# Strided attention blocks transposed in pairs, their value products on both row halves, and a smaller first transfer

## The chip, the cores and the metric

The kernel runs on one core of a Trainium2 chip. The metric is device time in microseconds (us) of one execution; lower is better. TensorE is PE in the profile (PEld is its weight load), VectorE is DVE, ScalarE is ACT, GpSimd is POOL and SyncE is SP.

## The reference

Three layers follow one another; all of it is float32, with batch 4, 8 heads, 576 positions, head size 64, model width 512 and hidden width 1024.

```
scores = where(mask, q k^T / sqrt(64), -1e9); attn = softmax(scores); x = attn v
    heads 0-3, local:   0 <= i - j < 32
    heads 4-7, strided: i >= j and i % 32 == j % 32
xk, xr = mixes of x and x shifted by one position
x2 = sigmoid(xr w_r) * (relu(xk w_k)^2 w_v)
h = relu(x2 w_in); out = (h * sigmoid(conv3(h))) w_out
```

## The kernel before, in words

Only the blocks of scores that the masks leave are computed. A local head has 9 blocks of 64 queries by 96 keys. For a strided head the positions are regrouped by remainder: 3 remainders of 18 positions make one block of 54 by 54, and a head has 11 of these. Heads go in pairs `p` (0 and 1 local, 2 and 3 strided), one head on partitions 0 to 63, the other on 64 to 127. A pair is worked in two units (`unit`, L359): 5 and 4 blocks if local, 6 and 5 if strided. So there are 8 units in each of the 4 batches, 4 of them strided.

The steps of a unit are: scores into one PSUM bank (L389), mask and row minimum on DVE (L402), exponentials on ACT (L407), sums and normalisation on DVE (L420 to L422), one transpose of each block on PE (L429) in two sections with one PSUM bank ("tr", of which there are two) each, a copy of each section to `pt` in SBUF (L432, by the helper's L258 on ACT or L260 on DVE), the value products into the one "pv" bank (L439), and the copy of their result into `xT` (L444 local; `place`, L456 and L458, strided). In a strided unit the value products contract over 54 rows, which all lie on partitions 0 to 53; `vt` holds v for one half of the blocks, so that a strided pair has two loads of it.

The two layers behind it split each float32 operand into a high and a low float32r part and take three products; these products (`mm`, L529, then `hh` L738 and `oo` L770) are most of PE's work. Weights come as 64-bit words and are narrowed by integer operations on DVE (L278 to L280) and ACT or DVE (L273, L275).

The order of the first part (attention and the layer with w_k, w_v and w_r) is written by a planner (`Plan`, L64): it gives each job the time that constants in the code say, and always takes the job that can start first. Jobs that ACT or DVE can do go to the one that is free first; from `PREFER_FROM` of the planner's time on, DVE has a handicap of 0.5. Each engine then executes its own list in that order. While nothing else is there at the beginning, PE does idle products ("stir", L648): `WARM` of them first, then some in gaps. The input transfer of the first pair is cut in two, so that the first unit's data come first (L344, L346). The second part (w_in, convolution, w_out) is a plan of its own.

Of the kernel before, what the change touches and what calls it, by code (L numbers as in the profile page):

```python
# [14 lines left out]
P = 128  # L15
# [20 lines left out]
BANKED = {"sc", "tr", "pv", "mm"}  # L36
RIGHT = {"raw", "wt", "wb", "qk", "vt", "pr", "nmx", "sums", "rec", "pt"}
# [168 lines left out]
def block_kernel(ctx, tc, qkL, qkS, vL, vS, mu_k, mu_r, w_k, w_v, w_r, w_in, conv_w, w_out, ident, mask_l, mask_s, out):  # L206
# [152 lines left out]
    def unit(b, p, half, loaded):  # L359

# [5 lines left out]
        if local:  # L366
            masks = [ml_sb[:, 0 if first + j == 0 else 1] for j in range(nb)]
            mask = fixed["ml"]
            qo = [LQ * j if half == 0 else LQ * LB[0] + S + STRIDE + LQ * j for j in range(nb)]
            ko = [LQ * LB[0] + LQ * (first + j) for j in range(nb)]  # L370
# [12 lines left out]
        pt = space(at, "pt", [P, SB[0] * SR], bufs=2, parts=2)  # L383

        def scores(e, blocks):
            for j in blocks:
                for ab in range(2):
                    r = slice(64 * ab, 64 * ab + 64)
                    pe.matmul(bank()[r, j * nk:(j + 1) * nk], qk()[r, qo[j]:qo[j] + LQ], qk()[r, ko[j]:ko[j] + nk], start=True, stop=True)  # L389

        reads = [(qk, 0)] if local and not half else [qk]
        cost = 0.025 + nk * 0.00065
        if b == 0 and p == 0 and half == 0:
            for s_ in range(2):
                plan.add({"PE": len(sections[s_]) * cost}, lambda e, s_=s_: scores(e, sections[s_]), reads, [(bank, s_)])
        else:
            first_scores.append(plan.add({"PE": nb * cost}, lambda e: scores(e, range(nb)), reads, [bank]))
        for s_, blocks in enumerate(sections):
            def masked(e, blocks=blocks):
                for i in blocks:  # L400
                    k = slice(i * nk, (i + 1) * nk)
                    dve.tensor_tensor_reduce(pr()[:, k], bank()[:, k], masks[i], -1.0 / 8.0, 3.0e38, ALU.add, ALU.min, nmx()[:, i:i + 1])  # L402

            def exps(e, blocks=blocks):
                for i in blocks:
                    k = slice(i * nk, (i + 1) * nk)
# [3 lines left out]
            plan.add({"DVE": m * (0.077 + nk / 960)}, masked, [(bank, s_), mask], [(pr, s_), (nmx, s_)])  # L410
            j = plan.add({"ACT": m * (0.29 + nk / 1400)}, exps, [(pr, s_), (nmx, s_)], [(pr, s_), (sums, s_)], table="exp")
            if unit_before[0]:
                plan.order(unit_before[0], j)
            unit_before[0] = j

        def normalise(e):
            x = pr()[:, :nb * nk].rearrange("p (n k) -> p n k", n=nb)
# [5 lines left out]
        for s_, blocks in enumerate(sections):  # L423
            turned = space(ps, "tr", [P, 512], bufs=BANKS["tr"])
            m = len(blocks)

            def turn(e, blocks=blocks, turned=turned):
                for j, i in enumerate(blocks):
                    pe.transpose(turned()[:nk, j * rows:(j + 1) * rows], pr()[:rows, i * nk:(i + 1) * nk], id_sb[:rows, :rows])  # L429

            plan.add({"PE": m * 0.098}, turn, [(pr, s_), fixed["id"]], [turned])
            copy(lambda blocks=blocks: pt()[:nk, blocks[0] * rows:(blocks[-1] + 1) * rows], lambda m=m, turned=turned: turned()[:nk, :m * rows], m * rows, [turned], [(pt, s_)])  # L432
        out_ = space(ps, "pv", [P, 512], bufs=BANKS["pv"])

        def values(e):
            for j in range(nb):
                for ab in range(2):
                    r, o = slice(64 * ab, 64 * ab + 64), j * rows + 64 * ab
                    pe.matmul(out_()[r, j * nq:(j + 1) * nq], vt()[:nk, j, r], pt()[:nk, o:o + nq], start=True, stop=True)  # L439

        plan.add({"PE": nb * (0.025 + nq * 0.00055)}, values, [vt, pt], [out_])
        x, n = xT[b], nb * nq
        if local:
            copy(lambda: x()[:, p, 1 + first * nq:1 + (first + nb) * nq], lambda: out_()[:, :n], n, [out_], [(x, 2 * p + half)])  # L444
        else:

            groups = [(0, nb, 0)] if half == 0 else [(0, nb - 1, 0), (nb - 1, 1, 1)]

            def place(e):
                dst = x()[:, p, 1:].rearrange("p (i r) -> p i r", r=STRIDE)  # L450
                src_ = out_()[:, :n].rearrange("p (n i g) -> p n i g", n=nb, i=NI)
                for j0, m, g0 in groups:
                    r0 = 3 * (first + j0)
                    d = dst[:, :, r0:r0 + m * (3 - g0)].rearrange("p i (n g) -> p n i g", n=m)
                    if e == "ACT":
                        act.activation(d, src_[:, j0:j0 + m, :, g0:], AF.Copy)  # L456
                    else:
                        dve.tensor_copy(d, src_[:, j0:j0 + m, :, g0:])  # L458

            plan.add({"ACT": 0.085 * len(groups) + n / 1400, "DVE": 0.065 * len(groups) + n / 960}, place, [out_], [(x, 2 * p + half)])  # L460

    def attention(b):
        xT[b] = space(wa, f"xT{b}", [P, KT, S + 1], tag="xT", bufs=2, parts=9)
# [352 lines left out]
def _layout(inputs):  # L816
# [9 lines left out]
        return np.ascontiguousarray(a.transpose(0, 1, 3, 2)).reshape(B, H // 4, 2 * D, -1)  # L826


    h, n0 = H // 2, LQ * LB[0]
# [9 lines left out]
    vS = v[:, h:, order].reshape(B, 2, 2, sum(SB), SQ, D).transpose(0, 1, 4, 3, 2, 5)  # L839
    vS = np.ascontiguousarray(vS).reshape(B, 2, SQ, sum(SB), 2 * D)  # L840

    t, i = np.arange(LK)[None, :], np.arange(2 * LQ)[:, None] % LQ
    near = (t > i) & (t <= i + STRIDE)
# [41 lines left out]
```

## Time and profile before

| what | us |
|---|---|
| median of 3 runs | 551.56 (550.79 to 551.92) |
| the profiled execution, its own time | 550.77 |
| its span, first to last instruction | 549.0 |
| PE busy | 536.0 |
| DVE busy | 362.3 |
| ACT busy | 350.8 |

The profile describes one execution. 1.77 us of its own time lie outside the span. A busy PE is not a PE at its peak: matmuls are pipelined, and a row's duration overlaps the next one's. What a step costs PE is therefore read from the chain of waits or from the distance of starts, not from the mean duration.

### The profile page before, as it was taken

To read this page: it belongs to the slowest core of one execution; us is meant where nothing else is said; L and a number is where in the kernel's file an instruction comes from. 1 tells how busy PE (TensorE), PEld (TensorE's weight loads), DVE (VectorE), ACT (ScalarE), POOL (GpSimd) and SP (SyncE) were. 2 spreads that over 40 slices of the span, in tenths; PEclk is the share of its full clock that TensorE was granted. 3 is DMA by queue.
4 is the path that set the end of the run, shared out by engine and by line. 5 is a ranking of instruction groups with operands and counts; after the bars stand their busy time and mean duration, and the time that the engine had idled before them with its cause. 6 is when DMAs were issued, how large, how long until landed. Compare 5 with 4: busy or idle time off the path is not lost.

```text
span 549.0 us, 11874 instructions
## 1 busy us (share of the span) xinstructions
PE 536.0 (98%) x4596; PEld 502.5 (92%) x4596; DVE 362.3 (66%) x999; ACT 350.8 (64%) x966; POOL 1.2 (0%) x15
## 2 busy tenths in 40 slices
PE   6989999999999999999999999999999999999997
PEld 5778999999999999999999999999899999998885
DVE  3999999778878757712655621699976755556510
ACT  5879998779948879927679562556554433433320
POOL 0000000000000000000000000000000000000000
PEclk9999999999999999999999999999999999999999
DMA  9764655794297440000230520323121010000011
GB/s 293 245 203 153 197 170 175 219 294 145 83 285 252 149 136 2 23 23 2 70 101 2 164 82 24 101 62 99 45 100 63 19 39 20 19 21 24 36 39 57
DMA packets 35208, 58.13 MB, mean 106 GB/s; under 512 B 3312, under 2 KB 22256, under 8 KB 35152
## 3 DMA queue, kind: packets, MB, share of 16 engines
q1 hardware_dynamic: 34576, 57.06, 32.9%
q8 instruction: 36, 0.59, 0.5%
q10 hardware_dynamic: 576, 0.32, 0.2%
q14 instruction: 20, 0.16, 0.1%
HBM read 43.74 MB, written 13.63 MB: 104 GB/s over the span
## 4 chain that ended last, share of the span: by engine, by line
PE 91%; DVE 4%; ACT 3%; DMA 1%; issue 1%; ACTq 0%
PE mm L529 44%; PE hh L738 18%; PE oo L770 18%; PE sc L389 4%; PE pv L439 3%; PE tr L429 3%; ACT pr L407 1%; DVE mx L509 1%; DVE wt L280 1%; DMA qk<-in_qkL 1%; DVE pr L402 1%; DVE wt L279 0%; ACT mx L508 0%; DVE Y L511 0%; ACT wb L273 0%
## 5 line engine op out<-in xcount | busy, mean ns | idle before, releaser
L529 PE MATMUL mm<-X,wvh 128*128 128x288 f32 x448 | 84.8, 299 | 0.0
L529 PE MATMUL mm<-Y,wkh 128*128 128x288 f32 x384 | 68.4, 296 | 0.0
L529 PEld LDWEIGHTS mm<-X,wvh 128*128 128x128 f32 x448 | 66.9, 188 | 0.5
L407 ACT ACTIVATE pr<-pr,nmx 128x54 f32<-128x54 f32 (+1 forms) x160 | 54.9, 348 | 9.4 <-DVE nmx L402 9.1
L529 PEld LDWEIGHTS mm<-Y,wkh 128*128 128x128 f32 x384 | 56.9, 188 | 0.0
L529 PE MATMUL mm<-Y,wrh 128*128 128x288 f32 x256 | 54.8, 299 | 0.6 <-DVE Y L511 0.4
L738 PE MATMUL hh<-x2h,wil 128*128 128x288 f32 x256 | 54.7, 295 | 0.0
L738 PE MATMUL hh<-x2l,wih 128*128 128x288 f32 x256 | 54.6, 294 | 0.0
L738 PE MATMUL hh<-x2h,wih 128*128 128x288 f32 x256 | 54.3, 293 | 0.0
L749 DVE SCALAR_TENSOR_TENSOR c<-hb,cw_sb,c 128x576 f32<-128x576 f32 x64 | 52.1, 818 | 1.4
L738 PEld LDWEIGHTS hh<-x2h,wih 128*128 128x128 f32 x256 | 43.9, 188 | 4.3
L529 PE MATMUL mm<-X,wvl 128*128 128x288 f32 x224 | 47.8, 295 | 0.0
L750 ACT ACTIVATE c<-c 128x576 f32<-128x576 f32 x32 | 21.9, 684 | 40.6 <-DVE c L749 40.5
L576 DVE TENSOR_TENSOR X<-sq,X 128x288 fp32r<-128x288 f32 x48 | 21.7, 458 | 35.1 <-ACT X L574 28.3
L529 PEld LDWEIGHTS mm<-Y,wrh 128*128 128x128 f32 x256 | 42.0, 188 | 1.6 <-DVE Y L511 0.6
L529 PE MATMUL mm<-Y,wkl 128*128 128x288 f32 x192 | 41.1, 295 | 0.0
L738 PEld LDWEIGHTS hh<-x2l,wih 128*128 128x128 f32 x256 | 41.0, 188 | 0.0
L738 PEld LDWEIGHTS hh<-x2h,wil 128*128 128x128 f32 x256 | 40.9, 188 | 0.0
L529 PE MATMUL mm<-Y,wrl 128*128 128x288 f32 x128 | 38.0, 297 | 0.4 <-DVE wrl L319 0.4
L746 ACT ACTIVATE hb<-hh 128x576 f32<-128x576 f32 x32 | 20.8, 651 | 24.4 <-PE hh L738 24.2
L529 PEld LDWEIGHTS mm<-X,wvl 128*128 128x128 f32 x224 | 35.9, 188 | 0.0
L751 DVE TENSOR_TENSOR c<-hb,c 128x576 f32<-128x576 f32 x32 | 24.3, 758 | 15.1 <-ACT c L750 14.6
(107 smaller groups left out, 1152.1 us busy)
## 6 DMA issues: line engine op xcount, KB each, us to landing
qk<-in_qkS SPq DMA_DIRECT2D x8, 599.0 KB
x_d<-rs SPq DMA_DIRECT2D x32, 144.0 KB
x2r<-x_d SPq DMA_DIRECT2D x8, 576.0 KB
out<-ob SPq DMA_DIRECT2D x17, 256.0 KB
qk<-in_qkL SPq DMA_DIRECT2D x7, 592.0 KB
raw<-in_w_k SPq DMA_DIRECT2D x8, 512.0 KB
raw<-in_w_v SPq DMA_DIRECT2D x8, 512.0 KB
raw<-in_w_in SPq DMA_DIRECT2D x8, 512.0 KB
```

What stands on the lines that cost most here:

```text
L389: pe.matmul(bank()[r, j * nk:(j + 1) * nk], qk()[r, qo[j]:qo[j] + LQ], qk()[r, ko[j]:ko[j] + nk], start=True, stop=True)
L407: act.activation(pr()[:, k], pr()[:, k], AF.Exp, bias=nmx()[:, i:i + 1], scale=-1.0, accum_out=sums()[:, i:i + 1])
L429: pe.transpose(turned()[:nk, j * rows:(j + 1) * rows], pr()[:rows, i * nk:(i + 1) * nk], id_sb[:rows, :rows])
L439: pe.matmul(out_()[r, j * nq:(j + 1) * nq], vt()[:nk, j, r], pt()[:nk, o:o + nq], start=True, stop=True)
L529: pe.matmul(o(), w_cols(name, j, t, part), x_[t](), start=(t == 0 and part == 0 and x_ is xhi), stop=(t == nk - 1 and x_ is xlo))
L576: plan.add({"DVE": 0.37}, lambda e: dve.tensor_tensor(l_(), sq(), h_().bitcast(F32), ALU.subtract), [sq, h_], [l_])
L738: pe.matmul(o()[:, i, :T], w()[:, t * P:(t + 1) * P], x_()[:, i, t], start=(t == 0 and w is whi and x_ is hi), stop=(t == KT - 1 and x_ is ...
L746: plan.add({"ACT": 0.54}, lambda e: act.activation(h()[:, 1:1 + S].rearrange("p (i t) -> p i t", i=2), o()[:, :, :T], AF.Relu), [o], [h])
L749: plan.add({"DVE": 0.735}, lambda e, k=k: dve.scalar_tensor_tensor(c(), h()[:, k:k + S], cw_sb[:, k * NF + f:k * NF + f + 1], c(), ALU.mul ...
L750: plan.add({"ACT": 0.6}, lambda e: act.activation(c(), c(), AF.Sigmoid), [c], [c], table="sigmoid")
L751: plan.add({"DVE": 0.67}, lambda e: dve.tensor_tensor(c(), h()[:, 1:1 + S], c(), ALU.mult), [h, c], [c])
L770: pe.matmul(o(), x_()[:, f, col:col + P], wsp["wo", f][part](), start=(f == 0 and x_ is th and part == 0), stop=(f == NF - 1 and x_ is tl))
```

## The change

Five things change.

- Strided units: a gap is left in `pr`, so that a block begins every 64 columns, and one transpose takes two neighbouring blocks (118 columns in, 118 rows out). A unit has 3 transposes, in one bank with one section, instead of 6 or 5 in two. The even blocks come out on rows 0 to 53, the odd ones on rows 64 to 117. The copy to `pt` has 118 rows (a unit of 5 blocks has a second one for its last block).
- Value products of a strided unit: the even blocks first, from rows 0 to 53 into the "pv" bank, then the odd ones from rows 64 to 117 into the bank that held the transposes. `place` copies from both banks, in 2 instructions (3 in a unit of 5 blocks) instead of 1 (2). The "tr" bank is held until then.
- v of a strided pair is laid out over 128 partitions, one transfer of 384 KB instead of two of 162 and 135 KB.
- The beginning: the first transfer has the queries of 3 blocks instead of 5 (416 columns instead of 672); the first unit's two sections have a bank of scores each; 10 idle products instead of 6, and idle products in gaps from 5 us of the plan on instead of 6.
- The planner's constants for scores, transposes and value products change, and `PREFER_FROM` goes from 30 to 20.

```diff
-WARM, MIXES, BEHIND = 6, 2, (0, 3)
+WARM, MIXES, BEHIND = 10, 2, (0, 3)
-PREFER, PREFER_FROM, BESIDE, SWITCH = 0.5, 30.0, 0.3, 0.09
+PREFER, PREFER_FROM, BESIDE, SWITCH = 0.5, 20.0, 0.3, 0.09
-LQ, LK, LB = 64, 96, (5, 4)
+LQ, LK, LB, LEAD = 64, 96, (5, 4), 3
...
-            cut = 2 * LQ * LB[0] + STRIDE
+            cut = 2 * LQ * LEAD + STRIDE
...
-        vt = [space(at, "vt", [P, 6, P], bufs=4) for _ in range(2)]
-        for h in range(2):
-            dma(lambda h=h: vt[h]()[:SQ, :SB[h]], lambda h=h: vS[b, p - 2, :, SB[0] * h:SB[0] * h + SB[h]], SQ * 4 * P * SB[h], [], [vt[h]])
-        return qk, vt
+        vt = space(at, "vt", [P, 6, P], bufs=4)
+        dma(vt, lambda: vS[b, p - 2], P * 4 * P * 6, [], [vt])
+        return qk, [vt, vt]
...
-        bank = space(ps, "sc", [P, 512], bufs=BANKS["sc"], parts=2)
+        early = b == 0 and p == 0 and half == 0
+        banks = [space(ps, "sc", [P, 512], bufs=BANKS["sc"], parts=2) for _ in range(1 + early)]
...
+        gap = nk if local else LQ
...
-        cost = 0.025 + nk * 0.00065
+        cost = 0.033 + nk * 0.00167
...
+            pairs = [(2 * i, SR if 2 * i + 1 < nb else SQ) for i in range(n0)]
+            def turn(e):
+                for i, n in pairs:
+                    pe.transpose(turned()[:n, i // 2 * SR:(i // 2 + 1) * SR], pr()[:SR, i * gap:i * gap + n], id_sb[:SR, :SR])
+            plan.add({"PE": n0 * 0.1}, turn, [pr, fixed["id"]], [turned])
+            both = nb // 2 * SR
+            def turned_out(e):
+                for n, k in ((SR, slice(0, both)), (SQ, slice(both, n0 * SR))):
+                    if k.start < k.stop:
...
         out_ = space(ps, "pv", [P, 512], bufs=BANKS["pv"])
+        outs_ = [out_] if local else [out_, turned]
...
+            for odd in range(2):
+                rows = slice(64 * odd, 64 * odd + SQ)
+                for i in range((nb - odd + 1) // 2):
+                    for ab in range(2):
+                        r, o = slice(64 * ab, 64 * ab + 64), i * SR + 64 * ab
+                        pe.matmul(outs_[odd]()[r, i * nq:(i + 1) * nq], vt()[rows, 3 * half + i, r], pt()[rows, o:o + nq], start=True, stop=True)
-        plan.add({"PE": nb * (0.025 + nq * 0.00055)}, values, [vt, pt], [out_])
+        plan.add({"PE": nb * (0.146 if local else 0.105)}, values, [vt, pt], outs_)
...
-            groups = [(0, nb, 0)] if half == 0 else [(0, nb - 1, 0), (nb - 1, 1, 1)]
+                for odd in range(2):
+                    m = (nb - odd + 1) // 2
+                    last = half == 1 and odd == 0
+                    groups = [(0, m - 1, 0), (m - 1, 1, 1)] if last else [(0, m, 0)]
...
-                    if stirred and 6.0 < start < STIR_UNTIL and job.room:
+                    if stirred and 5.0 < start < STIR_UNTIL and job.room:
```

## Rows read from the trace of the kernel before

**Rows 1.** Windows: length, then busy us (instructions) of each engine, clock, DMA share, GB/s.

```profile
20.00:30.00 10.00, 9.40 (x163) 7.16 (x160) 9.71 (x47) 8.82 (x35) 0.00 (x0) 1.00 0.66 197
30.00:40.00 10.00, 8.24 (x79) 7.04 (x74) 10.00 (x27) 7.64 (x15) 0.00 (x0) 1.00 0.71 207
...
60.00:130.00 70.00, 69.75 (x780) 66.86 (x777) 60.50 (x216) 61.46 (x214) 0.26 (x1) 1.00 0.66 204
```

**Rows 2.** Chain of waits, 60 to 300 us: start, us, what (xinstructions).

```profile
by line: PE mm L529 79.8%; PE pv L439 7.3%; PE sc L389 5.9%; PE tr L429 5.7%; DVE mx L509 0.4%; DVE pr L402 0.3%; ACT wb L273 0.3%; ACT pt L258 0.3%; issue 0.1%; DVE nmx L402 0.0%
...
97.09 0.72 PE sc L389 x20
...
98.55 0.84 PE sc L389 x24
...
105.86 0.98 PE mm L529 x6
...
112.81 0.84 PE pv L439 x24
...
114.64 0.72 PE pv L439 x20
...
116.08 0.80 PE mm L529 x6
...
187.25 0.30 PE tr L429 x3
```

**Rows 3.** Groups by line and form, weight loads of local and strided transposes.

```profile
L429 PEld LDWEIGHTS tr<-id_sb,pr 128*96 128x96 f32 x72 | 8.0, 125 | 1.3 <-ACT pt L258 1.0
L429 PEld LDWEIGHTS tr<-id_sb,pr 118*54 118x54 f32 x88 | 7.9, 106 | 2.2 <-ACT pr L407 0.5 <-DVE pr L418 0.5
```

**Rows 4.** Windows of the instructions on tr, where the stretches from 60 us hold 120.

```profile
60.00:130.00 70.00, 6.67 (x45) 4.59 (x45) 0.00 (x0) 6.02 (x16) 1.00 0.66 204
130.00:170.00 40.00, 0.38 (x2) 0.25 (x2) 1.37 (x3) 0.00 (x0) 1.00 0.59 186
170.00:220.00 50.00, 6.76 (x45) 4.66 (x45) 2.29 (x5) 4.33 (x11) 1.00 0.38 119
...
260.00:290.00 30.00, 4.26 (x28) 2.68 (x28) 1.80 (x4) 3.04 (x8) 1.00 0.26 79
```

**Rows 5.** Groups by line and form, copies of transposes and of products in strided units.

```profile
L258 ACT ACTIVATE pt<-tr 54x354 f32<-54x354 f32 x18 | 7.6, 453 | 1.2 <-PE tr L429 1.0
...
L456 ACT ACTIVATE xT<-pv 128x324 f32<-128x324 f32 x7 | 3.5, 497 | 3.6 <-PE pv L439 3.6
L456 ACT ACTIVATE xT<-pv 128x216 f32<-128x216 f32 x8 | 3.1, 382 | 2.7 <-PE pv L439 2.5
...
L258 ACT ACTIVATE pt<-tr 54x236 f32<-54x236 f32 x6 | 2.1, 354 | 2.0 <-PE tr L429 2.0
...
L456 ACT ACTIVATE xT<-pv 128x36 f32<-128x36 f32 x8 | 1.5, 192 | 0.0
```

**Rows 6.** Timeline of the first 13 us, all engines: start, us, engine, line, what.

```profile
1.12 1.62 PE L648 MATMUL scrap<-idle 128*128 128x288 bf16 x6 [1.12 <-POOL xT L464]
...
4.37 3.14 PE L389 MATMUL sc<-qk 64*64 64x96 f32 x36 [1.63 <-DMA qk<-in_qkL]
...
6.28 0.26 DVE L402 CUSTOM_DVE_ANT_0 pr<-sc,ml_sb 128x96 f32<-128x96 f32 x1 [6.28 <-PE sc L389]
...
8.72 1.70 PE L389 MATMUL sc<-qk 64*64 64x96 f32 x36
```

**Rows 7.** Window of the fourth us, columns as in the first group.

```profile
3.00:4.00 1.00, 0.00 (x0) 0.00 (x0) 0.00 (x0) 0.41 (x1) 0.00 (x0) 1.00 1.04 379
```

**Rows 8.** Timeline of DVE and PE, 21 to 33 us: one strided unit's way, and the first `mm`.

```profile
21.24 0.76 PE L429 MATMUL tr<-id_sb,pr 118*54 118x118 f32 x6 [0.26 <-ACT pr L407]
...
27.25 0.51 DVE L458 COPY xT<-pv 128x324 f32<-128x324 f32 x1 [0.28 <-PE pv L439]
...
32.29 0.39 PE L529 MATMUL mm<-Y,wrh 128*128 128x288 f32 x1
```

More of the change, by code (lines that the diff above doesn't have):

```diff
@@ L368, in unit @@
             mask = fixed["ml"]
-            qo = [LQ * j if half == 0 else LQ * LB[0] + S + STRIDE + LQ * j for j in range(nb)]
-            ko = [LQ * LB[0] + LQ * (first + j) for j in range(nb)]
+            qo = [LQ * j + (S + STRIDE) * (j >= LEAD) for j in range(first, first + nb)]
+            ko = [LQ * LEAD + LQ * (first + j) for j in range(nb)]
         else:
@@ L377, in unit @@
         sections = [range(n0), range(n0, nb)]
-        bank = space(ps, "sc", [P, 512], bufs=BANKS["sc"], parts=2)
+        early = b == 0 and p == 0 and half == 0
+        banks = [space(ps, "sc", [P, 512], bufs=BANKS["sc"], parts=2) for _ in range(1 + early)]
+        bank_of = [banks[early * (i >= n0)] for i in range(nb)]
+        at_ = [(i - n0 * (early and i >= n0)) * nk for i in range(nb)]
         pr = space(at, "pr", [P, LB[0] * LK], bufs=3, parts=2)
@@ L388, in scores @@
                     r = slice(64 * ab, 64 * ab + 64)
-                    pe.matmul(bank()[r, j * nk:(j + 1) * nk], qk()[r, qo[j]:qo[j] + LQ], qk()[r, ko[j]:ko[j] + nk], start=True, stop=True)
-        reads = [(qk, 0)] if local and not half else [qk]
-        cost = 0.025 + nk * 0.00065
-        if b == 0 and p == 0 and half == 0:
+                    pe.matmul(bank_of[j]()[r, at_[j]:at_[j] + nk], qk()[r, qo[j]:qo[j] + LQ], qk()[r, ko[j]:ko[j] + nk], start=True, stop=True)
+        cost = 0.033 + nk * 0.00167
+        if early:
             for s_ in range(2):
-                plan.add({"PE": len(sections[s_]) * cost}, lambda e, s_=s_: scores(e, sections[s_]), reads, [(bank, s_)])
+                plan.add({"PE": len(sections[s_]) * cost}, lambda e, s_=s_: scores(e, sections[s_]), [(qk, range(1 + s_))], [banks[s_]])
         else:
-            first_scores.append(plan.add({"PE": nb * cost}, lambda e: scores(e, range(nb)), reads, [bank]))
+            first_scores.append(plan.add({"PE": nb * cost}, lambda e: scores(e, range(nb)), [qk], banks))
         for s_, blocks in enumerate(sections):
@@ L400, in masked @@
                 for i in blocks:
-                    k = slice(i * nk, (i + 1) * nk)
-                    dve.tensor_tensor_reduce(pr()[:, k], bank()[:, k], masks[i], -1.0 / 8.0, 3.0e38, ALU.add, ALU.min, nmx()[:, i:i + 1])
+                    dve.tensor_tensor_reduce(pr()[:, i * gap:i * gap + nk], bank_of[i]()[:, at_[i]:at_[i] + nk], masks[i], -1.0 / 8.0, 3.0e38, ALU.add, ALU.min, nmx()[:, i:i + 1])
             def exps(e, blocks=blocks):
                 for i in blocks:
-                    k = slice(i * nk, (i + 1) * nk)
+                    k = slice(i * gap, i * gap + nk)
                     act.activation(pr()[:, k], pr()[:, k], AF.Exp, bias=nmx()[:, i:i + 1], scale=-1.0, accum_out=sums()[:, i:i + 1])
             m = len(blocks)
-            plan.add({"DVE": m * (0.077 + nk / 960)}, masked, [(bank, s_), mask], [(pr, s_), (nmx, s_)])
+            plan.add({"DVE": m * (0.077 + nk / 960)}, masked, [(banks[0], s_) if not early else banks[s_], mask], [(pr, s_), (nmx, s_)])
             j = plan.add({"ACT": m * (0.29 + nk / 1400)}, exps, [(pr, s_), (nmx, s_)], [(pr, s_), (sums, s_)], table="exp")
@@ L416, in normalise @@
         def normalise(e):
-            x = pr()[:, :nb * nk].rearrange("p (n k) -> p n k", n=nb)
+            x = pr()[:, :nb * gap].rearrange("p (n k) -> p n k", n=nb)[:, :, :nk]
             dve.tensor_tensor(x, x, rec()[:, :nb].unsqueeze(2).to_broadcast([P, nb, nk]), ALU.mult)
@@ L422, in unit, with turn @@
         plan.add({"DVE": 0.075 + nb * nk / 960}, normalise, [pr, rec], [pr])
-        for s_, blocks in enumerate(sections):
-            turned = space(ps, "tr", [P, 512], bufs=BANKS["tr"])
[L425 to L432, printed above, removed]
+        if local:
+            for s_, blocks in enumerate(sections):
+                turned = space(ps, "tr", [P, 512], bufs=BANKS["tr"])
+                m = len(blocks)
+                def turn(e, blocks=blocks, turned=turned):
+                    for j, i in enumerate(blocks):
+                        pe.transpose(turned()[:nk, j * P:(j + 1) * P], pr()[:, i * nk:(i + 1) * nk], id_sb)
+                plan.add({"PE": m * 0.108}, turn, [(pr, s_), fixed["id"]], [turned])
+                copy(lambda blocks=blocks: pt()[:nk, blocks[0] * P:(blocks[-1] + 1) * P], lambda m=m, turned=turned: turned()[:nk, :m * P], m * P, [turned], [(pt, s_)])
+        else:
+            turned = space(ps, "tr", [P, 512], bufs=BANKS["tr"])
+            pairs = [(2 * i, SR if 2 * i + 1 < nb else SQ) for i in range(n0)]
[7 more added lines that the diff above has]
+                    if k.start < k.stop:
+                        if e == "ACT":
+                            act.activation(pt()[:n, k], turned()[:n, k], AF.Copy)
+                        else:
+                            dve.tensor_copy(pt()[:n, k], turned()[:n, k])
+            one = 1 + nb % 2
+            plan.add({"ACT": 0.085 * one + n0 * SR / 1400, "DVE": 0.065 * one + n0 * SR / 960}, turned_out, [turned], [pt])
@@ L433, in unit @@
         out_ = space(ps, "pv", [P, 512], bufs=BANKS["pv"])
+        outs_ = [out_] if local else [out_, turned]
         def values(e):
[L436 to L439, printed above, removed]
-        plan.add({"PE": nb * (0.025 + nq * 0.00055)}, values, [vt, pt], [out_])
+            if local:
+                for j in range(nb):
+                    for ab in range(2):
+                        r, o = slice(64 * ab, 64 * ab + 64), j * P + 64 * ab
+                        pe.matmul(out_()[r, j * nq:(j + 1) * nq], vt()[:nk, j, r], pt()[:nk, o:o + nq], start=True, stop=True)
+                return
+            for odd in range(2):
+                rows = slice(64 * odd, 64 * odd + SQ)
+                for i in range((nb - odd + 1) // 2):
+                    for ab in range(2):
+                        r, o = slice(64 * ab, 64 * ab + 64), i * SR + 64 * ab
+                        pe.matmul(outs_[odd]()[r, i * nq:(i + 1) * nq], vt()[rows, 3 * half + i, r], pt()[rows, o:o + nq], start=True, stop=True)
@@ L445, in unit @@
         else:
-            groups = [(0, nb, 0)] if half == 0 else [(0, nb - 1, 0), (nb - 1, 1, 1)]
             def place(e):
                 dst = x()[:, p, 1:].rearrange("p (i r) -> p i r", r=STRIDE)
[L451 to L460, printed above, removed]
+                for odd in range(2):
+                    m = (nb - odd + 1) // 2
+                    src_ = outs_[odd]()[:, :m * nq].rearrange("p (n i g) -> p n i g", n=m, i=NI)
+                    last = half == 1 and odd == 0
+                    groups = [(0, m - 1, 0), (m - 1, 1, 1)] if last else [(0, m, 0)]
+                    for j0, c_, g0 in groups:
+                        r0 = 3 * (first + 2 * j0 + odd)
+                        if c_ == 1:
+                            d = dst[:, :, r0:r0 + 3 - g0].rearrange("p i (n g) -> p n i g", n=1)
+                        else:
+                            d = dst[:, :, r0 - 3 * odd:r0 - 3 * odd + 6 * c_].rearrange("p i (n h g) -> p h n i g", n=c_, h=2)[:, odd]
+                        v = src_[:, j0:j0 + c_, :, g0:]
+                        if e == "ACT":
+                            act.activation(d, v, AF.Copy)
+                        else:
+                            dve.tensor_copy(d, v)
+            plan.add({"ACT": 0.085 * (2 + half) + n / 1400, "DVE": 0.065 * (2 + half) + n / 960}, place, outs_, [(x, 2 * p + half)])
     def attention(b):
@@ L826, in heads_t @@
         return np.ascontiguousarray(a.transpose(0, 1, 3, 2)).reshape(B, H // 4, 2 * D, -1)
-    h, n0 = H // 2, LQ * LB[0]
+    h, n0 = H // 2, LQ * LEAD
     lead = np.zeros((B, H // 4, 2 * D, STRIDE), q.dtype)
@@ L838, in _layout @@
     vL = np.ascontiguousarray(vL).reshape(B, 2, LK, sum(LB), 2 * D)
-    vS = v[:, h:, order].reshape(B, 2, 2, sum(SB), SQ, D).transpose(0, 1, 4, 3, 2, 5)
-    vS = np.ascontiguousarray(vS).reshape(B, 2, SQ, sum(SB), 2 * D)
+    vo = v[:, h:, order].reshape(B, 2, 2, sum(SB), SQ, D).transpose(0, 1, 4, 3, 2, 5).reshape(B, 2, SQ, sum(SB), 2 * D)
+    vS = np.zeros((B, 2, P, 6, 2 * D), v.dtype)
+    vS[:, :, :SQ] = vo[:, :, :, 0::2]
+    vS[:, :, LQ:LQ + SQ, :5] = vo[:, :, :, 1::2]
     t, i = np.arange(LK)[None, :], np.arange(2 * LQ)[:, None] % LQ
```

2 lines of the change are left out of this document (1 added, 1 removed).

## Prediction

> **What bounds the kernel now.** Begin with the busy times: PE is busy for 536.0 of 549.0 us, DVE and ACT for about two thirds. A share over the whole span hides stages, so the windows come next. From 60 us on PE is the bound: it is busy for 69.75 of 70 us between 60 and 130, while DVE and ACT have 9 us to spare [rows 1]. Between 20 and 40 us it is DVE, with 9.71 and 10.00 of each 10 us; ACT has 8.82 and 7.64 [rows 1]. The chain of waits says the same for 60 to 300 us: four PE lines hold 98.7% of it and the other engines 1.3%, some 3.1 us [rows 2]. The second part of the kernel is not touched and has no part in this.
>
> So two prices hold. From 60 us on, a microsecond of PE work removed is a microsecond of time, and work on ACT or DVE costs nothing as long as it is not late. Before the first `mm` product at 32.29 us [rows 8], PE waits for the attention of batch 0 and the mixes behind it; there a step counts if it shortens the way through DVE and ACT, and PE instructions cost nothing.
>
> **Transposes.** There are 88 strided ones (the weight loads of 54 columns [rows 3]), 22 in each batch. The stretches from 60 us hold 45 + 2 + 45 + 28 = 120 transposes [rows 4], which is 40 for each of three batches: 18 local and 22 strided. So 66 strided ones lie where PE is the bound. The change makes 12 of each 22; 30 go away there. Their price is read from the chain, 3 in 0.30 us, or 0.10 each [rows 2]. The pair transpose streams the same 118 columns of the identity, so I price it the same: **-3.0 us**. What grows is its weight load, 118 columns for 54. Loads took 106 ns with 54 and 125 ns with 96 columns [rows 3], 0.45 ns a column, so some 135 ns with 118. If the 29 ns more were not hidden behind the stream, 36 pair transposes would give back 1.0 us; but the loads of 96 columns are hidden in the same way, since PE is as full where local units run. Bounds -2.0 and -3.0. The 10 that go in batch 0 lie before 32 us and count nothing.
>
> **Value products.** Their number and shapes stay; the odd blocks move to rows 64 to 117. A unit of 6 blocks took 0.84 and one of 5 took 0.72 us, so one block more costs 0.12 us [rows 2]. Does the other row half help? The scores of 54 columns tell: there the two heads lie on different row halves, and the same two sizes took 0.84 and 0.72 us [rows 2]. In the value products the heads share one row half and differ in columns alone. Equal prices for both say that the row half is not what limits; and the change issues all even blocks, then all odd ones, so that the halves meet once in a unit. I take **0**. Bounds: if the halves ran beside each other wholly, 66 blocks at 0.06 us less, -4.0; if the seam between them cost what leaving a half-array stretch costs (six `mm` in 0.98 against 0.80 us [rows 2], 0.18), 12 units, +2.2.
>
> The Trainium skill, "TensorEngine Tiling (Array Packing)", section Theoretical Speedup, gives up to 2x where the contracted dimension is at most 64. By it the sum would be lower by those 4.0 us; the equal rows speak against it here.
>
> **The beginning.** Before, DVE's first instruction starts at 6.28 us and waits for PE's scores [rows 6]. They begin at 4.37, and 36 instructions took 3.14 us, 0.087 each [rows 6]. A block is 4 instructions (two heads, each product in two); five blocks end at 4.37 + 1.74 = 6.11, which with 0.17 of latency is 6.28. So DVE waited for the whole bank of five blocks, not for its section of three. With a bank for each section it waits for 12 instructions, 1.05 us: 0.69 us earlier. The smaller transfer has 256 columns less, 131 KB, at 379 GB/s [rows 7] 0.35 us. Together 1.0 us earlier. Does that reach 32 us? ACT and DVE are nearly full on the way, so mostly. But there are only two score banks, and the first unit now takes both: the second unit's scores (4 blocks, 1.4 us at 0.087) no longer follow at once, but wait until DVE has read the first section, and DVE and ACT may wait for them in turn. I leave a third of the gain to that and take **-0.7**; bounds 0 (the shift is lost in a later wait) and -1.0. Ten idle products instead of six are 2.7 us at 0.27 each [rows 6]; from 1.12 they end at 3.8, before the data would come at 4.0, so they cost nothing. The first scores ran at 0.087 an instruction, those from 8.72 us at 0.047 (36 in 1.70) [rows 6]. PE idled for 1.63 us before the former [rows 6]; with that gap nearly closed the first 12 might run at the faster rate, 0.5 us. The granted clock reads 1.00 in these windows, so the rows cannot tell; it stays in the range.
>
> **Copies.** A unit of 6 blocks loses one copy to `pt` (453 ns) and splits one copy to `xT` (497 ns) in two [rows 5]. Those of 216 and 36 elements took 382 and 192 ns, 1.06 ns an element [rows 5]; two of 162 are 0.65 us. Net -0.30. A unit of 5 had 453 + 354 + 382 + 192 = 1381 ns [rows 5] and gets 354 + 255 (118 columns, at the 0.84 ns between 236 and 354) + 268 + 268 + 192 = 1337. So a pair saves 0.34 us of ACT or DVE, batch 0 0.69. Spread over two nearly full engines: **-0.35**; bounds 0 and -0.7. From 60 us on it is hidden behind PE; without that cover it would be a gain again.
>
> **Transfers.** v of a strided pair is 87 KB more, 174 KB in batch 0: 0.46 us at 379 GB/s [rows 7]. It comes after the data that are waited for, and SP issues one transfer fewer in each pair: 0, bounds 0 and +0.5.
>
> **The planner.** Its prices for scores and value products roughly double, and from 20 us copies lean to ACT. Both reorder the whole first part. What could go well is that the 3.1 us of other engines in the chain [rows 2] vanish; what could go badly is as much again. Between 20 and 40 us DVE is the fuller engine and ACT has 3.5 us to spare [rows 1], so the lean to ACT should not hurt. I take 0, bounds -3.1 and +3.1.
>
> **Sum.** -3.0 - 0.7 - 0.35 = -4.05. Against the profiled execution's own 550.77 us (span 549.0 and 1.77 around it) that is 546.7. The median of the runs stands 0.8 higher, by which it is 547.5. I predict 547.0, between them. The likeliest case's own range is 544.8 to 549.2.
>
> **Rivals.**
> 1. The odd half runs beside the even one. For it: different rows, different banks. Against it: equal prices of scores and value products [rows 2], and the order of issue. 547.0 - 4.0 = 543.0.
> 2. The work goes but the time doesn't: the new order brings as much waiting as PE loses work. For it: PE already waits at places for DVE and ACT [rows 2]. Against it: 9 us of slack on both in 70 [rows 1]. +4.0 on the forecast, 551.0.
> 3. Slower: the transposes' bank becomes the bound. It is now held until `place` has read the odd products. The first strided unit of batch 0 took from its transposes at 21.24 to the end of its `xT` copy at 27.76, 6.5 us [rows 8]. With two banks that is one unit in 3.3 us and 13 us for four, where the four took from 21.2 to the first `mm` at 32.3, 11.1. That adds some 2 us in each batch in which PE has no `mm` products ready to fill with; behind PE's transpose, which waits in order, everything else on PE stands. With two batches hit it costs 4 and only eats the gain; from three it decides: four batches, 547.0 + 8 = 555. Against it: most of the 6.5 us is waiting for a place in the order, which a shorter unit (one copy instead of two) needs less of.
>
> **How the numbers follow.** The likeliest 0.60, rival 1 0.13, rival 2 0.14, rival 3 0.10, and 0.03 for an order that wins the whole 3.1 us. Under 0.2%, 1.1 us, no measurement of this kernel can tell two times apart. Faster is the likeliest, rival 1 and the last, with a little of rival 2: 0.78; same is most of rival 2, 0.12; slower is rival 3, 0.10. The range goes from rival 1's 543.0 to rival 2's 551.0, which leaves out rival 3 and some of what lies below 543, under 2 in 10.
>
> **What would show it.** Right: 48 strided transposes with starts some 0.10 us apart; value products of 6 blocks still at 0.84 us; DVE's first instruction near 5.2 us and the first `mm` near 31; PE as full as before after 60 us, and the first part's end some 4 us earlier. Wrong: value products at 0.4 to 0.5 us (rival 1); more steps of other engines in the chain after 60 us (rival 2); PE's transposes waiting for copies to `xT` (rival 3); a first `mm` no earlier than 32.3, by which the beginning's part falls.

## The result, and the profile after

The changed kernel takes 544.67 us (543.75 to 545.84, 4 runs); the kernel before, timed beside it on the same chip, 551.46 us (550.79 to 551.92, 4 runs). The ratio is 0.9879 with a 95% interval of 0.9853 to 0.9905, or 6.8 us less. A second measurement on another chip gave 0.9876 (0.9855 to 0.9897). So the sign and the range of the forecast hold. Its point, 547.0, lies 2.3 us above the time.

The profiled execution took 543.75 us, with a span of 542.0 us against 549.0. First the page of the changed kernel: busy times, then the clock in 40 slices.

```profile
PE 530.9 (98%) x4545; PEld 499.0 (92%) x4545; DVE 356.2 (66%) x982; ACT 348.2 (64%) x987; POOL 1.2 (0%) x15
...
PEclk9888999999999999999999999999999999999999
```

PE is 5.1 us less busy than before, and the clock, 1.00 in [rows 1], now falls short of it in three early slices.

The timelines of PE place the end of the first part, which is the first `hh` product. Before:

```profile
344.72 0.43 PE L738 MATMUL hh<-x2h,wih 128*128 128x288 f32 x2
```

After:

```profile
337.73 0.43 PE L781 MATMUL hh<-x2h,wih 128*128 128x288 f32 x2
```

That is 7.0 us earlier, as much as the span is shorter. So everything happened in the first part, and the question is where in it. The chain of waits from 60 us to that product, grouped by line, answers it. Before, over 284.72 us:

```profile
by line: PE mm L529 83.0%; PE pv L439 6.1%; PE sc L389 5.0%; PE tr L429 4.8%; DVE mx L509 0.3%; DVE pr L402 0.3%; ACT wb L273 0.2%; ACT pt L258 0.2%; issue 0.1%; DVE nmx L402 0.0%
```

After, over 277.73 us:

```profile
by line: PE mm L572 85.7%; PE sc L395 5.0%; PE pv L468 3.0%; PE tr L434 2.0%; PE tr L445 1.8%; PE pv L476 1.4%; PE tr L476 1.0%; issue 0.0%
```

Multiply each share by its window. L434 are local transposes, L445 pair transposes, L468 local value products. L476 are the strided value products: even blocks go into `pv` and odd ones into the bank called `tr`, so they have two names. The chain gives DVE or ACT some stretches in which PE still works at something else. The last column therefore counts PE alone from the same two traces: each product is charged the time from the end of the one before it to its own end, and time without a product is a wait.

| us | chain before | chain after | difference | PE alone, difference |
|---|---|---|---|---|
| transposes | 13.7 | 10.6 | -3.1 | -3.6 |
| value products | 17.4 | 15.0 | -2.4 | -2.3 |
| DVE, ACT and issue; PE's waits | 3.1 | 0 | -3.1 | -1.1 |
| `mm` products | 236.3 | 238.0 | +1.7 | +1.0 |
| scores | 14.2 | 13.9 | -0.3 | -1.1 |

The chain's differences add up to -7.2 (a share is rounded to 0.1%, 0.28 us), those of PE alone to -7.0 before rounding. On PE alone the strided transposes go from 7.9 to 5.0 us, -3.0, and the strided value products from 9.3 to 6.9, -2.4. The rest of the row of transposes is five local ones that the new order has already done by 60 us.

The `mm` products grew for a reason that the windows of their instructions give. Before, from 0 to 60 us:

```profile
0.00:60.00 60.00, 23.00 (x156) 21.05 (x156) 1.00 0.71 225
```

After:

```profile
0.00:60.00 60.00, 22.99 (x143) 21.32 (x144) 0.91 0.73 233
```

13 products fewer were done by 60 us, at 0.133 each (six in 0.80, [rows 2]) 1.7 us. But of the scores there are fewer left. Their windows from 60 us to the first `hh`, before:

```profile
60.00:344.72 284.72, 16.52 (x400) 1.00 0.39 121
```

After:

```profile
60.00:337.73 277.73, 16.38 (x364) 1.00 0.39 125
```

36 scores (0.036 each, 20 in 0.72 [rows 2]) and five local transposes (0.11 each) more are done, some 1.9 us. So at 60 us the changed kernel is about level with the one before, not ahead of it. This is one execution: the profile of the second measurement, an execution of 547.19 us, starts `mm` at 30.70 us, has done 127 products by 60 us and comes to the first `hh` at 341.17. So a difference of some 3 us between two profiled executions need not come from an edit.

**Transposes and value products**, in the chain of waits of the changed kernel (start, us, what):

```profile
107.15 0.30 PE tr L445 x3
...
109.58 0.45 PE tr L445 x3
```

A pair transpose costs 0.10 us behind `mm` products, the price of [rows 2] for half as many blocks. Right behind scores three take 0.15 more, near the 0.18 that six `mm` products show behind a half-array stretch in [rows 2]. The weight loads grew to a median of 137 ns and stay hidden. The timeline of PE over one value-product unit of 6 blocks, 24 instructions:

```profile
108.18 0.38 PE L476 MATMUL pv<-pt,vt 54*64 54x54 f32 x6
108.35 0.27 PE L476 MATMUL tr<-pt,vt 54*64 54x54 f32 x2
108.40 0.23 PE L476 MATMUL pv<-pt,vt 54*64 54x54 f32 x2
108.45 0.22 PE L476 MATMUL tr<-pt,vt 54*64 54x54 f32 x1
...
108.57 0.25 PE L395 MATMUL sc<-qk 64*64 64x96 f32 x1
...
108.68 0.22 PE L476 MATMUL tr<-pt,vt 54*64 54x54 f32 x2
```

All twelve even products are issued before the first odd one, yet an odd one (`tr`) starts at 108.35 with six even ones still to come. From there to the last even one at 108.52 the two halves run together, just under a third of the unit. At 108.57 the next unit's first score starts ahead of the last odd products. In the chain the unit holds PE from 108.25 to 108.85, 0.60 us for the 0.84 of [rows 2]; the next unit, of 5 blocks, holds it from 111.63 to 112.16, 0.53 for 0.72. Where `mm` products follow, nothing of the next job is mixed in:

```profile
266.16 0.38 PE L476 MATMUL pv<-pt,vt 54*64 54x54 f32 x6
...
266.82 0.40 PE L572 MATMUL mm<-X,wvh 128*128 128x288 f32 x1
```

From first start to next job's first start that is 0.66 us for 24 instructions; before, such a unit (112.74 to 113.58) took 0.84.

**The copies**, in the groups by line and form (count, busy us, mean ns, idle before):

```profile
L454 ACT ACTIVATE pt<-tr 118x354 f32<-118x354 f32 x8 | 3.7, 460 | 0.5 <-PE tr L445 0.2
...
L499 ACT ACTIVATE xT<-tr 128x162 f32<-128x162 f32 x8 | 2.6, 328 | 0.0
...
L499 ACT ACTIVATE xT<-pv 128x162 f32<-128x162 f32 x8 | 2.6, 323 | 0.8 <-PE pv L476 0.8
```

A unit of 6 blocks has 460 + 328 + 323 = 1111 ns for 2 x 453 + 497 = 1403 [rows 5]. The forecast was a net 0.30 less; it is 0.29. A unit of 5 has 361 + 255 + 281 + 272 + 199 = 1368 ns, for a forecast of 1337.

**The beginning**, in the timeline of the changed kernel:

```profile
4.95 0.26 DVE L406 CUSTOM_DVE_ANT_0 pr<-sc,ml_sb 128x96 f32<-128x96 f32 x1 [4.95 <-PE sc L395]
...
24.46 1.67 PE L395 MATMUL sc<-qk 64*64 64x96 f32 x17 [2.12 <-issue]
...
28.74 0.59 PE L572 MATMUL mm<-Y,wrh 128*128 128x288 f32 x1
```

DVE starts 1.33 us earlier than in [rows 6], and the first `mm` 3.55 us earlier than in [rows 8]. But PE stands idle for 2.12 us up to 24.46, and the windows (PE's, PEld's, DVE's, ACT's and POOL's busy us, then the clock) show what came next:

```profile
22.00:24.00 2.00, 0.34 (x3) 0.09 (x2) 2.00 (x12) 2.00 (x11) 0.00 (x0) 1.00 1.09 322
24.00:26.00 2.00, 1.54 (x22) 1.57 (x23) 2.00 (x9) 2.00 (x5) 0.00 (x0) 0.53 1.10 236
...
28.00:30.00 2.00, 2.00 (x20) 1.90 (x15) 0.94 (x6) 1.91 (x9) 0.00 (x0) 0.50 0.91 274
...
42.00:44.00 2.00, 2.00 (x10) 2.00 (x10) 2.00 (x9) 1.49 (x3) 0.00 (x0) 0.50 0.08 26
```

From 24 to 30 us PE runs at 1.2 GHz, the lower of its levels (0.50), so the early `mm` products cost almost twice the usual: six in the chain at 29.07 us take 1.46 for 0.80. The clock falls a second time: it reads 0.80, 0.50 and 0.85 in the three windows from 40 to 46 us, behind a window (38 to 40) in which PE was busy for 0.81 of 2 us. From 42 to 44 us PE is full and does 10 instructions, from 46 to 48, at 1.00, 17.

### The profile page after: what moved, and what is told of

Read it like the earlier page. It is cut to its first block, busy times and chain, and to the rows that moved or that the text cites. A ratio compares the mean times of both kernels' runs of the same rounds, so it can differ in the third digit from the quotient of the medians.

```text
span 542.0 us, 11750 instructions
## 1 busy us (share of the span) xinstructions
PE 530.9 (98%) x4545; PEld 499.0 (92%) x4545; DVE 356.2 (66%) x982; ACT 348.2 (64%) x987; POOL 1.2 (0%) x15
## 4 chain that ended last, share of the span: by engine, by line
PE 92%; ACT 4%; DVE 2%; issue 1%; POOL 0%; ACTq 0%; POOLq 0%
PE mm L572 45%; PE hh L781 19%; PE oo L813 18%; PE sc L395 4%; PE pv L468 2%; PE tr L445 1%; PE tr L434 1%; PE pv L476 1%; DVE pr L406 1%; ACT pr L411 1%; ACT mx L551 1%; PE tr L476 1%; PE scrap L691 0%; ACT wb L273 0%; ACT rs L589 0%
## 5 line engine op out<-in xcount | busy, mean ns | idle before, releaser
L572 PEld LDWEIGHTS mm<-Y,wrh 128*128 128x128 f32 x256 | 43.4, 195 | 3.1 <-ACT Y L553 1.3
```

Of the source, the lines that this page charges most:

```text
L572: pe.matmul(o(), w_cols(name, j, t, part), x_[t](), start=(t == 0 and part == 0 and x_ is xhi), stop=(t == nk - 1 and x_ is xlo))
```

## The experiments

Three things could explain 6.8 us. The first theory is the prediction's: PE's saved work, with a small gift of the beginning. The rival says that the planner's constants, costed at nothing, carry much of it through the order of the work. A third question is what the fallen clock cost. Ratios are to the kernel before on the same chip; 0.002 is 1.1 us.

**The beginning alone**, put on the kernel before:

```diff
-WARM, MIXES, BEHIND = 6, 2, (0, 3)
+WARM, MIXES, BEHIND = 10, 2, (0, 3)
...
+LQ, LK, LB, LEAD = 64, 96, (5, 4), 3
...
+        banks = [space(ps, "sc", [P, 512], bufs=BANKS["sc"], parts=2) for _ in range(1 + early)]
...
-                    if stirred and 6.0 < start < STIR_UNTIL and job.room:
+                    if stirred and 5.0 < start < STIR_UNTIL and job.room:
```

> The kernel before with the beginning alone: three blocks in the first transfer, a bank for each section, ten idle products. Theory A (the time comes after 60 us: 3.8 us less PE work and 3.1 us of waits that are gone; what the beginning wins is lost again before 60 us): DVE starts near 5.0 us, but the time is within 1 us of before, 550.5 to 551.5. Rival B (the beginning gives 3 to 3.5 us, as the first mm product 3.5 us earlier says): 548 to 548.5.

Measured: 551.94 us (12 runs) against 551.33, ratio 1.0017 (1.0003 to 1.0031). DVE starts at 5.15 instead of 6.28, the first `mm` at 32.16 instead of 32.29. The shift of 1.1 us is lost on the way; the beginning is worth nothing here: by the interval the kernel is 0.2 to 1.7 us slower, its median a little above theory A's range.

**The strided units alone**, with the beginning and the constants of before. Against the changed kernel:

```diff
-PREFER, PREFER_FROM, BESIDE, SWITCH = 0.5, 20.0, 0.3, 0.09
+PREFER, PREFER_FROM, BESIDE, SWITCH = 0.5, 30.0, 0.3, 0.09
...
-LQ, LK, LB, LEAD = 64, 96, (5, 4), 3
+LQ, LK, LB, LEAD = 64, 96, (5, 4), 5
...
-        cost = 0.033 + nk * 0.00167
+        cost = 0.025 + nk * 0.00065
...
-        plan.add({"PE": nb * (0.146 if local else 0.105)}, values, [vt, pt], outs_)
+        plan.add({"PE": nb * (0.025 + nq * 0.00055)}, values, [vt, pt], outs_)
```

> The kernel before with the strided units alone (pair transposes, value products on both row halves, v over 128 partitions), the planner's old constants. Theory A: only the 3.8 us of PE work go, 547.5, and waits of 2 to 3 us stay in the chain after 60 us. Rival B (the strided units are the 3.5 us that the beginning does not give): 548, no different from A in time; rival C (the waits went because units are shorter): 544.5 to 545.

Measured: 548.2 us (8 runs), ratio 0.9944 (0.9924 to 0.9963), 3.1 us less. The saved work is the same as in the changed kernel: on PE alone, the strided transposes and value products after 60 us take 12.0 us here, 11.9 in the changed kernel and 17.2 before. Of these 5.3 us not all reaches the time. PE's waits from 60 to 337 us (what it waited for, us, times, longest) show where it stands instead:

```profile
PE sc L393 <- DVE nmx L404: 0.9, 1, 0.9
PE mm L570 <- ACT wvh L318: 0.5, 1, 0.5
...
```

These and three of 0.4 us are 2.6 us; the kernel before has 1.2 in the same view and the changed kernel none.

**The constants alone**, on the kernel before:

```diff
-PREFER, PREFER_FROM, BESIDE, SWITCH = 0.5, 30.0, 0.3, 0.09
+PREFER, PREFER_FROM, BESIDE, SWITCH = 0.5, 20.0, 0.3, 0.09
...
-        cost = 0.025 + nk * 0.00065
+        cost = 0.033 + nk * 0.00167
...
-        plan.add({"PE": nb * (0.025 + nq * 0.00055)}, values, [vt, pt], [out_])
+        plan.add({"PE": nb * (0.146 if local else 0.105)}, values, [vt, pt], [out_])
```

> The kernel before with the planner's constants alone (scores, transposes, value products, the lean to ACT from 20 us). Theory A: the same PE work, but no waits in the chain after 60 us, so 3 us less: 548.4. Rivals B and C (the constants do nothing by themselves): 551.5, within 1 us.

Measured: 549.41 us (6 runs), ratio 0.9963 (0.9945 to 0.998), 2.0 us less. Not one instruction of the computation differs here; only the order does, the share of ACT and DVE, and the idle products (19 for 36). In the profiled execution PE's waits after 60 us are 0.8 us for 1.2, so waits that go, the reason in theory A, are the smaller part; by 60 us PE has done 36 scores and five local transposes more and six `mm` products fewer, an estimated 1.1 us.

**Idle products in the gap at 22 us**, in the changed kernel. The place where it may put them waits for a bank that isn't free there, so 17 go into the bank of the first idle products:

```diff
+                        elif 20.0 < start < 28.0 and start - pe_end > 1.0:
+                            stir(int((start - pe_end) / 0.13), scrap)
```

> The changed kernel with some 17 idle products in the gap of 2.1 us at 22.3 us, into a bank that is not yet in use. If the half clock from 24 to 31 us costs time: the granted clock stays at 1.00 there and the time is 1 to 2 us lower, 543. If PE is not what is waited for there: clock 1.00 and the same time, 544.7 within 0.7.

Measured: 543.68 us (6 runs), ratio 0.9873 (0.9844 to 0.9901). Its windows show the clock kept:

```profile
24.00:26.00 2.00, 1.97 (x23) 1.45 (x23) 2.00 (x14) 2.00 (x8) 0.00 (x0) 1.00 1.11 260
...
28.00:30.00 2.00, 2.00 (x32) 1.76 (x32) 2.00 (x7) 2.00 (x12) 0.00 (x0) 1.00 0.92 254
...
42.00:44.00 2.00, 2.00 (x10) 2.00 (x10) 1.96 (x4) 1.08 (x4) 0.00 (x0) 0.50 0.02 4
```

The first `hh` starts at 337.99, no earlier than without them (337.73). PE at half its clock from 24 to 31 us cost nothing measurable; that DVE and ACT (2.00 of 2.00 here) set the pace at that place fits, and by 60 us only five `mm` products more are done (148 for 143). The second fall, from 40 to 46 us, is still there. No run takes it alone away, and what it costs is not settled; an estimate from 10 instructions for 17 in 2 us, over some 3.4 us, is 1.6 us of PE's work.

**The changed kernel again**, on the chip of the next three:

> The changed kernel once more, beside the other kernels of this call on the same chip: 544.7, within 1 us.

Measured: 543.81 us (6 runs), ratio 0.9876 (0.9855 to 0.9897).

**Strided units and constants, without the beginning**: the strided kernel above, with the new prices and `PREFER_FROM` at 20.

> The changed kernel without its beginning (five blocks in the first transfer, one score bank for the first unit, 6 idle products): strided units and constants together. Theory A (the strided units take 3.8 us off PE after 60 us, the constants take the waits away, the beginning gives nothing): 544.7, the same as the changed kernel within 1 us. Rival B (the beginning is worth 2 us once units and constants are there): 546.5 to 547. Rival D (the effects only add, -3.1 and -1.9 as measured alone): 546.4.

Measured: 543.93 us (4 runs), ratio 0.9872 (0.9855 to 0.9889), 7.1 us less. The changed kernel is no better than this, so the beginning is worth nothing beside the rest either. And -7.1 is 2.0 us more than the two parts had alone, -3.1 and -2.0; with some 1 us of interval on each of the three, that is only just clear of noise. Its profiled execution (544.89 us) has PE waits after 60 us in spite of the new prices, as many as the strided units alone:

```profile
PE sc L393 <- DVE nmx L404: 2.1, 2, 1.2
PE pv L474 <- ACT pt L452: 0.6, 1, 0.6
```

**Even and odd products in turn**, so that neighbours in the issue order lie on different row halves:

```diff
-            for odd in range(2):
-                rows = slice(64 * odd, 64 * odd + SQ)
-                for i in range((nb - odd + 1) // 2):
+            for i in range(n0):
+                for odd in range(1 + (2 * i + 1 < nb)):
+                    rows = slice(64 * odd, 64 * odd + SQ)
```

> The changed kernel with even and odd blocks issued in turn, not all even ones first. If the halves of the rows overlap only as far as the order lets them: a unit of 6 blocks falls from 0.60 us to between 0.4 and 0.5, 1.2 to 2.4 us less after 60 us, 542.5 to 543.5. If PE starts the odd ones ahead of the even ones anyway, or another limit holds at 25 ns an instruction: 0.60 as before and the same time within 0.7 us.

Measured: 543.6 us (5 runs), ratio 0.9858 (0.9839 to 0.9876). The timeline of PE in this kernel, a unit of 6 blocks:

```profile
265.76 0.26 PE L476 MATMUL pv<-pt,vt 54*64 54x54 f32 x2
265.77 0.27 PE L476 MATMUL tr<-pt,vt 54*64 54x54 f32 x2
265.86 0.23 PE L476 MATMUL pv<-pt,vt 54*64 54x54 f32 x2
...
266.10 0.22 PE L476 MATMUL tr<-pt,vt 54*64 54x54 f32 x2
266.26 0.53 PE L572 MATMUL mm<-X,wvh 128*128 128x288 f32 x2
```

Pairs on the two halves start 0.01 to 0.02 us apart, every four instructions take 0.06, and from its first start to the next job's the unit takes 0.50 us instead of 0.66. On PE alone the strided value products after 60 us take 5.9 us instead of 6.9: a saving of 1.0, not of the 2 that was expected. PE's waits after 60 us are 1.0 us, and the changed kernel has none. The first `hh` starts at 337.58 against 337.73, and the time's interval overlaps that of the changed kernel.

**Local transposes with weight loads of 128 columns** in place of 96, but for the last block of a unit (the rows beyond 96 of the result aren't read), in the changed kernel, one run:

```diff
-                        pe.transpose(turned()[:nk, j * P:(j + 1) * P], pr()[:, i * nk:(i + 1) * nk], id_sb)
+                        m_ = P if i + 1 < nb else nk
+                        pe.transpose(turned()[:m_, j * P:(j + 1) * P], pr()[:, i * nk:i * nk + m_], id_sb)
```

> The changed kernel with local transposes that load 128 columns where they loaded 96 (the neighbouring block's columns are turned too and not read); what they stream, 128 columns of the identity, stays. If the weight load sets the price of a transpose, these come at distances of 0.14 to 0.16 us instead of 0.11 and the time is some 2 us higher (42 of them after 60 us, 0.05 each), 546.7. If the streamed columns set it, 0.11 and the same time.

Measured: 544.09 us. Its chain of waits:

```profile
173.29 0.44 PE tr L435 x4
```

The changed kernel's chain has the same stretch:

```profile
172.96 0.44 PE tr L434 x4
```

0.11 us each in both. A third more columns in the load cost nothing, so a transpose's price here is not that of its load. The stream of the identity fits, 128 columns at 0.11 in the local units and 118 at 0.10 in the strided ones; no run changed it.

**The lean to ACT from 30 again**, in the changed kernel:

```diff
-PREFER, PREFER_FROM, BESIDE, SWITCH = 0.5, 20.0, 0.3, 0.09
+PREFER, PREFER_FROM, BESIDE, SWITCH = 0.5, 30.0, 0.3, 0.09
```

> The changed kernel with the lean to ACT from 30 us of the plan on, as before, all else changed. Strided units and constants together gave 2 us more than the two alone; this and the next run tell which constants do it. If the lean does: 546 to 547. If the prices do: 544, within 1 us of the changed kernel.

Measured: 543.26 us (4 runs), ratio 0.9857 (0.9841 to 0.9872). The lean brings nothing beside the new prices.

**The old prices**, in the changed kernel, with everything else new:

```diff
-        cost = 0.033 + nk * 0.00167
+        cost = 0.025 + nk * 0.00065
...
-        plan.add({"PE": nb * (0.146 if local else 0.105)}, values, [vt, pt], outs_)
+        plan.add({"PE": nb * (0.025 + nq * 0.00055)}, values, [vt, pt], outs_)
```

> The changed kernel with the planner's old prices for scores, transposes and value products (about half of what they take), the lean to ACT from 20 us kept. If the prices are worth what the constants gave beside the strided units: 547 to 548, and more idle products or more PE waits after 60 us. If the lean is: 544, within 1 us.

The transposes' prices go back too, to 0.098 each from 0.108 (local) and 0.1.

Measured: 550.11 us (4 runs), ratio 0.998 (0.9965 to 0.9994). That is more than the 547 to 548 expected. In this kernel the planner's prices for three kinds of jobs hold nearly the whole gain: on the same chip the kernel above, with the new prices, takes 543.26. PE's waits from 60 to 337 us:

```profile
PE sc L395 <- DVE nmx L406: 1.7, 1, 1.7
PE mm L572 <- DVE rs L629: 0.7, 1, 0.7
PE mm L572 <- DVE X L619: 0.6, 1, 0.6
PE mm L572 <- ACT Y L553: 0.4, 1, 0.4
PE mm L572 <- DVE Y L554: 0.4, 1, 0.4
```

The windows of two stretches with the old prices:

```profile
130.00:337.00 207.00, 204.15 (x1910) 198.88 (x1909) 115.87 (x371) 153.29 (x452) 0.11 (x1) 1.00 0.30 94
200.00:220.00 20.00, 18.25 (x194) 17.59 (x190) 11.92 (x45) 18.89 (x63) 0.00 (x0) 1.00 0.07 23
```

And the first of them in the changed kernel:

```profile
130.00:337.00 207.00, 207.00 (x1957) 202.68 (x1955) 113.07 (x366) 146.51 (x450) 0.11 (x1) 1.00 0.28 90
```

The chain of waits of the kernel with old prices shows the longest of the waits:

```profile
205.25 0.56 PE tr L434 x5
...
205.83 0.26 DVE pr L406
...
206.28 0.86 DVE mx L552 x2
...
207.54 0.79 PE sc L395 x20
```

A strided unit's scores wait 1.7 us for row minima on DVE. These begin only when PE's transposes are through, and in DVE's order two mixes, 0.86 us together, stand between them. DVE is idle for 8 of the 20 us: it is not too slow; the order is wrong at this place.

**In turn, and with idle products in the gap**: the two edits above together.

> The changed kernel with even and odd blocks in turn and with the idle products in the gap at 22 us, both. In turn a unit of 6 blocks took some 0.42 us instead of 0.60, 12 units after 60 us, 2 us; the warm clock at 24 us alone gave nothing clear. Theory: 542 to 543. Rival (what PE saves turns into waits): 543.7.

Measured: 543.48 us (4 runs), ratio 0.9851 (0.9828 to 0.9875).

**In turn, without the beginning**: strided units and constants, the products in turn, and 0.08 for 0.105 as their price.

> Strided units and constants with the old beginning, even and odd blocks in turn, and the planner told of it (0.08 us a block instead of 0.105). Theory: the old beginning costs nothing and the turn gives up to 2 us: 541.8 to 543. Rival (the saved PE work is waited away): 543.9.

Measured: 543.66 us (5 runs), ratio 0.9845 (0.9817 to 0.9874). Neither can be told apart from the changed kernel. PE stands for about 2.8 us after 60 us in this one, 1.8 of it at scores that wait for row minima. That is as much as in the kernel without the beginning and without the turn (2.7), so what became of the shorter products' 1 us is not shown here.

## Why the prediction was right, and where it was not

That the gain was this large is in part luck. With the planner's old prices the same faster step, beginning and lean measured 550.11 for 551.33 us, 1.2 less, and the prediction had put the change of prices at nothing.

**Transposes, -3.0: right**, by count and by price. PE alone gives -3.0 for the strided ones, 0.10 us a pair, and the larger load is hidden. The chain's -3.1 has five local transposes in it that were done before 60 us, some 0.5.

**Value products, 0: the term was mis-sized.** They gave -2.4 in the chain, between 0 and the -4.0 of the rival in which the halves run beside each other. The step that failed is "Equal prices for both say that the row half is not what limits; and the change issues all even blocks, then all odd ones, so that the halves meet once in a unit". Neither half of it holds. PE starts odd products before the even ones are through, so the halves run together for just under a third of the unit. And row halves in turn cost a quarter less again, 0.50 for 0.66. Why the scores, on two halves, were no cheaper before was not tried; both halves of theirs write one bank, and even and odd value products write two.
The Trainium skill, "TensorEngine Tiling (Array Packing)", section Theoretical Speedup, gives up to 2x: here the trace shows 0.84 to 0.66 us as the change issues them, a factor of 1.3, and 0.50 in turn, 1.7. The argument from equal rows was weaker than the rule.

**The beginning, -0.7: wrong in its reach, at the edge of its bounds (0 and -1.0).** DVE starts earlier by 1.33 us, a little more than forecast. But "ACT and DVE are nearly full on the way, so mostly" drew the wrong conclusion: the gain was gone by 60 us, where the two kernels are about level. Alone and beside the rest the beginning measured 0 or a little worse. The early first `mm` was no sign of a gain.

**Copies, -0.35:** their durations came out nearly as forecast. That they were worth something rests on the same reach to the first `mm`, and no run separates them.

**The planner's constants, 0 with bounds of 3.1: the largest error.** The step that failed is "Both reorder the whole first part", with a gain and a loss of 3.1 us taken as equally likely: what prices of half the true size do to an order was not worked out. Alone the constants give -2.0 us. Beside the strided units they give 4.0 (0.9944 to 0.9872, both without the beginning, on different chips), and with the beginning too, new prices for old, some 5.6 (0.998 to 0.9876 or 0.9879, on different chips). The lean is worth nothing beside the new prices, so in the changed kernel it is the prices; in the run of the constants alone the two are not separated. A unit's scores at 54 columns had 0.060 us a block in the plan and 0.12 in [rows 2]; its value products 0.055 and 0.12.
With such prices the plan lets PE come to a job earlier than it can, and other engines' results turn up late where PE is full. That this is why the order is worse is argued, not shown: one set of prices was measured against one other, with the same sign in three kernels.
What the worse order costs can be read in the changed kernel with old prices. Its profiled execution comes to the first `hh` at 344.19, 6.46 us later, with the same steps on PE and four `mm` products fewer left at 60 us. Both are single executions. After 60 us PE waits 4.0 us for 0.1. Behind six of these waits the first product ends some 0.26 us later than one in a stream, 1.6 us. And `mm` products start right behind scores or value products 17 times for 8, at 0.18 ([rows 2]) another 1.6. That is 7.1, less 0.5 for the four products: 6.6.
Waits alone do not tell a good order: the strided units have as many with the new prices (2.7 us) as with the old (2.6) where the beginning is left out, and still take 4.0 us less. An estimated 1.4 of these were won ahead of 60 us (44 scores and five local transposes more, six `mm` products fewer); the rest was not assigned. The prediction gave an order that wins the 3.1 us of other engines in the chain of [rows 2] a chance of 3 in 100. They are gone in the changed kernel, but on PE alone they were 1.1.

**The rivals.** The bank of the transposes never became the bound: the list of PE's waits after 60 us is empty. Saved work turned into waiting, as the second rival had it, with the old prices: without the beginning the strided units lose some 2.2 of their 5.3 us, with it 4.1. Against the profiled execution the sum came out 2.95 us too high (546.7 for 543.75). Counted on PE alone, it missed 2.4 us of value products, 1.1 of waits and some 1.7 of scores and local transposes that were done ahead of 60 us; against them stand 1.05 us of beginning and copies that did not arrive and 1.0 of `mm` work.

## What to carry to other kernels

Where a list scheduler writes the order, take its prices from distances between starts in the trace, and do this anew when a step changes its form: here that was worth about as much as the faster step, and without it 2.2 to 4.1 of the step's 5.3 us were lost. This rests on one set of prices against one other. Once an engine is full, count its work only from the point where it is full; here an earlier start upstream was worth nothing where two other engines were the bound in between, and so was a better clock from 24 to 31 us. Work moved to the other half of PE's rows overlapped even when it was issued behind the first half.

## What was not expected of the hardware

Matmuls on the other row half start ahead of matmuls issued before them (108.35 before 108.40 us in the timeline above), and scores of the next unit at 108.57 ahead of products at 108.68. A unit of 24 instructions in front of `mm` products takes 0.84 us on one half, 0.66 with one half issued behind the other and 0.50 in turn. After 2.12 us without work PE's granted clock was 0.53 and then 0.50 up to 30 us, though PE was busy for 1.54, 1.83 and 2.00 of each 2 us; it stood at 1.00 again from 32 to 40 us. From 40 to 46 it was 0.80, 0.50 and 0.85, behind 2 us in which PE was busy for 0.81.
